# Bucket-masked attention and two MoE blocks on one core: the second block's inner layer in two parts, the first part woven into the second batch's MoE

## The chip, the cores and the metric

One core of a Trainium2 chip runs the whole program. The metric is the device time of one execution in microseconds. Engines: TensorE (PE), VectorE (DVE), ScalarE (ACT), GpSimd (POOL), SyncE (SP, which only issues DMAs here).

## The reference

Three stages, in float32:

```python
# 1. attention; q, k, v: (2, 8, 768, 64); proj: (64, 6)
bucket(t) = sum(2**i * (t @ proj > 0)[i])               # 6 sign bits of q and k
mask   = bucket(q)[:, :, :, None] == bucket(k)[:, :, None, :]
scores = where(mask, q @ k.T / 8, -1e9)
attn   = softmax(scores) @ v                            # -> x: (2, 768, 512)
# 2. first MoE; w_in (512, 1024), w_spatial (768, 768), w_out (512, 512)
u, v   = split(relu(x @ w_in))
v_s    = w_spatial @ layernorm(v) + b_spatial           # over the sequence
x      = (u * v_s) @ w_out
# 3. second MoE; w_ch1 (512, 2048), w_ch2 (2048, 512)
out    = x + relu(layernorm(x) * g_ln @ w_ch1) @ w_ch2
```

The weights w_in, w_out, w_ch1 and w_ch2 arrive as float64.

## The kernel before

Every product that must be exact to float32 is made of three matmuls: an operand is split into a high and a low part in the format fp32r, and high x high, high x low and low x high are summed in PSUM (`mm3`, `PASSES`). The high part is a copy (ScalarE or GpSimd), the low part a subtraction (VectorE or GpSimd).

**Attention.** 96 tiles of 128 queries: two batches, eight heads, six tiles (three groups of two). `attn_step(i)` is a software pipeline: transposes of tile i, scores of tile i+2, masked maximum (VectorE) and exponential (ScalarE) of tile i+1, low parts of tile i (`e_lo`), weighted sum of the group before. The transposed exponentials come in two halves of three blocks: ScalarE copies the high part and VectorE subtracts, or, where `ES` says so for the second half, ScalarE copies to `es` and GpSimd makes both parts. Score tiles lie in two buffers of two PSUM banks, 384 columns in each; four more banks (`ps_b`) serve all else. Heads come in pairs; a pair's q and k are loaded, split, masked and copied nine to zero steps ahead (`pair_stages`, `AT`). SP issues all DMAs, in order.

**Conversions.** A float64 weight piece of 512 KB is loaded into a staging buffer (`stage_f64`, tag f64), and turned into fp32r halves: one ScalarE operation (line 103), five VectorE operations (104 to 108), GpSimd's join (112), ScalarE's high half (81) and GpSimd's low half (87). There is one staging buffer in the attention and two after it. The twelve pieces of w_in and w_out are made at the steps in `CONV_AT`, stored and reloaded for the second batch; the 32 pieces of w_ch1 and w_ch2 (`w1_piece`, `w2_piece`) later.

**First MoE** (`moe1`), a generator with 24 yields: six token tiles, 12 projections of 12 matmuls, then for each of six row tiles 18 spatial matmuls (pg), the gate (gt, VectorE), four transposes (ptr_g), and 12 output matmuls (py); each y is stored to DRAM. The first batch's runs inside the attention from step `M0` on; the second batch's follows the attention, with eight PSUM banks, and between its yields the first 11 conversions and the first LayerNorm chunk are put in as `SEQ` and `LNX` say.

**Second MoE.** Three chunks of 512 tokens (chunk 0, 1, 2). In step (c, f), f of 16, `up` makes 12 matmuls into pc, ScalarE the relu and VectorE the low part of ch; `down`, one step behind, makes 12 matmuls into four sums that stay open for a chunk. The remaining 21 conversions are put in two a step. At a chunk's end VectorE adds the residual and SP stores.

The framework that builds the program orders each engine's instructions by priority (the order in which they are written) and by its own estimate of when each is ready; every engine then runs its list in order. `issue_after` puts instructions behind a given one on its engine.

Of the kernel before, what the change touches and what calls it, by code (L numbers as in the profile page):

```python
# [17 lines left out]
P = 128  # L18
# [11 lines left out]
def attn_moe_kernel(ctx: ExitStack, tc: tile.TileContext, qT, kT, v, proj, w_in, w_spT, b_sp, w_out, g_ln, w1, w2, out):  # L30
# [13 lines left out]
    TB = 5  # L44
# [3 lines left out]
    CONV_AT = (4, 9, 14, 19, 24, 30, 34, 39, 55, 60, 66, 71)  # L48
# [4 lines left out]
    M0 = 50  # L53
    SPP = [(0, t) for t in range(6)]
    VNP = [(0, t) for t in range(6)]
    LNF = 7
# [4 lines left out]
    WARM = 28  # L61
    WARM2 = 16
    XB = 3
    AT = (-9, -8, -7, -4, 0)
    ES = (1, 0)
    SEQ = (2, 2, 4, 0, 2, 0, 0, 2, 0, 2, 0, 0, 0, 0, 1, 1, 0, 2, 3, 1, 0, 0, 1, 0)
    LNX = (14, 15, 19, 22)
# [6 lines left out]
    TCH = 512  # L74
    SCALE = 1.0 / float(D) ** 0.5
# [110 lines left out]
    def w_piece(src, nk, n, nm, lo, hl=None):  # L186

        st = mp.tile([P, nk, n], F32, tag="wst", name=f"wst_{nm}", bufs=1)
        nc.sync.dma_start(out=st, in_=src)
# [14 lines left out]
    def pair_load(b, r, which=(("k", kT), ("q", qT))):  # L204

        pr = pairs.setdefault((b, r), {})
        for nm, src in which:
            pr[nm] = ap.tile([P, 2, S], F32R, tag=nm + "2", name=f"{nm}2_{b}_{r}", bufs=1 if nm == "k" else 2)
            nc.sync.dma_start(
                out=pr[nm][:, LOW[nm]].bitcast(F32), in_=src[b, 2 * r : 2 * r + 2].rearrange("h d s -> (h d) s")  # L210
            )

    def pair_split(b, r, first=False):

        for nm in "kq":
            t = pairs[b, r][nm]
            hi, lo = t[:, 1 - LOW[nm]], t[:, LOW[nm]]
            raw = lo.bitcast(F32)
# [5 lines left out]
            if nm == "k" and not first:  # L224
                split_lo(lo, raw, hi)
# [3 lines left out]
    def mismatch(b, r):  # L229
# [3 lines left out]
        for c in range(2):  # L233
            csl = slice(c * KC, (c + 1) * KC)
            pm = ps_b.tile([P, 512], F32, tag="b", name=f"pm_{b}_{r}_{c}")
            for i, nm in enumerate("kq"):
                raw = pairs[b, r][nm][:, LOW[nm]].bitcast(F32)
# [48 lines left out]
    def scores(b, h, g, j):  # L286
# [3 lines left out]
        sc = ps_s.tile([P, 2, 512], F32, tag="sc", name=f"sc_{jm}")  # L290
        for c in range(2):
            for i, rows in enumerate((P, MR)):
                nc.tensor.matmul(  # L293
                    sc[:, c, :KC],
                    qs[:rows, i, qsl],
                    ks[:rows, i, c * KC : (c + 1) * KC],
                    start=(i == 0),
                    stop=(i == 1),
# [3 lines left out]
    def masked_max(b, h, g, j):  # L302
# [6 lines left out]
            x.rearrange("p (c k) -> p c k", c=2),  # L309
            t["sc"][:, :, :KC],  # L310
# [14 lines left out]
    def transposes(b, h, g, j):  # L325
# [7 lines left out]
        for c in range(2):  # L333
# [5 lines left out]
            if c == 1 and ES[(h * NTH + g * GRP + j) % len(ES)]:  # L339
                es = ap.tile([P, 3, P], F32, tag="es", name=f"es_{jm}", bufs=1)  # L340
# [136 lines left out]
    def conversions(pieces):  # L477

        res = []
        for key, nk, n, parts in pieces:  # L480
            for i, (src, ksl, fsl) in enumerate(parts):
# [11 lines left out]
                def finish(d=d, key=key, nk=nk, n=n, ksl=ksl, fsl=fsl, done=i == len(parts) - 1):  # L493
# [4 lines left out]
                    if done:  # L498
                        w_split[key] = dram.tile([P, 2, nk, n], F32, tag=f"ws_{key}", name=f"ws_{key}")
                        nc.sync.dma_start(out=w_split[key], in_=hl.bitcast(F32))  # L500
# [9 lines left out]
    def moe1(b, ps_m, tag):  # L510
# [84 lines left out]
        for t in range(NQT + 1):  # L595
# [15 lines left out]
            if t > 0:  # L611
# [7 lines left out]
                y = mp.tile([P, DM], F32, tag="tmp", name=f"y_{b}_{t - 1}", bufs=TB)  # L619
# [9 lines left out]
    ps_s = att.enter_context(tc.tile_pool(name="ps_s", bufs=2, space=PSUM))  # L629
    ps_b = att.enter_context(tc.tile_pool(name="ps_b", bufs=4, space=PSUM))  # L630
# [4 lines left out]
    pair_load(0, 0)  # L635
# [14 lines left out]
    for i in range(-1 - QA, NT + 3):  # L650
        attn_step(i)
        for e in pair_steps.get(i, ()):
            e()
# [8 lines left out]
        if i == M0:  # L662
            m0 = moe1(0, ps_b, "b")
        if m0 is not None:
            while n0 < (i - M0 + 1) * 24 / (NT - M0):
                next(m0, None)
                n0 += 1
    for _ in m0:
        pass
    att.close()  # L670
    N1A, N2A = 8, 3
    TPC = TCH // P
    NCH = B * S // TCH
    outv = out.rearrange("b (t p) d -> (b t) p d", p=P)
    w1t, w2t, xhs, accs, chs, xcs, mvs, rs = {}, {}, {}, {}, {}, {}, {}, {}

    def w1_piece(pool, f):
        w1t[f] = pool.tile([P, 2, KFT, P], F32R, name=f"w1t_{f}", bufs=1)
        load_f64(w1t[f][:, 0], w1t[f][:, 1], w1[:, :, f * P : (f + 1) * P], f"w1_{f}")

    def w2_piece(pool, f):
        w2t[f] = pool.tile([P, 2, 1, DM], F32R, name=f"w2t_{f}", bufs=1)
        load_f64(w2t[f][:, 0], w2t[f][:, 1], w2[:, f : f + 1, :], f"w2_{f}")

    def ln_stats(c, t):
        if t == 0:
            xcs[c] = [m2a.tile([P, DM], F32, tag="xc", name=f"xc_{c}_{i}", bufs=TPC) for i in range(TPC)]
            mvs[c] = m2a.tile([P, TPC, 2], F32, tag="mv", name=f"mv_{c}", bufs=2)
        xc = xcs[c][t]
        nc.sync.dma_start(out=xc, in_=y_dram[c * TPC + t])  # L690
# [9 lines left out]
    def ln_x(c, t, pool, ps, tag):  # L700
# [144 lines left out]
```

## Time and profile before

| | |
|---|---|
| median of 3 runs | 766.64 us (763.05 to 768.99) |
| profiled execution | 762.6 us |
| its span | 760.8 us |
| mean granted TensorE clock | 0.975 |
| TensorE, VectorE, ScalarE, GpSimd busy | 91%, 63%, 45%, 38% |
| instructions | 10493 |

The span is from the first to the last event that the profiler records; the execution's own time has 1.8 us more around it. Busy shares are means over stages with different limits. Rows of matmuls overlap, since they are pipelined, so their busy times exceed what they cost; the distance from start to start is what one costs.

### The profile page before, as it was taken

How to read it: one execution, taken by the hardware profiler on the slowest of the kernel's cores; microseconds unless marked ns; L12 is line 12 of the kernel's file. 1: busy time of each engine (PE TensorE's matmuls, PEld its weight loads, DVE VectorE, ACT ScalarE, POOL GpSimd, SP SyncE). 2: the span in 40 equal slices, each digit the busy share in tenths (PEclk: the TensorE clock that was granted, in tenths of full speed). 3: DMA queues.
4: the chain of work that ended last, by engine and by line, in shares of the span. 5: the costliest groups of instructions: out<-in, count | busy, mean ns of one | idle time of the engine just before them, and what ended most of it. 6: DMA issues, size and time to landing. Idle time of an engine off the chain costs nothing.

```text
span 760.8 us, 10493 instructions
## 1 busy us (share of the span) xinstructions
PE 692.0 (91%) x3588; PEld 578.2 (76%) x3588; DVE 482.1 (63%) x889; ACT 340.1 (45%) x679; POOL 291.8 (38%) x303
## 2 busy tenths in 40 slices
PE   5989888889989999999988887997899999999997
PEld 4877767778878978897766665865678888888885
DVE  2799989884978785564499895699974114221112
ACT  1777868584665865555345432333241112110110
POOL 3367665746565784232034453555542000000000
PEclk9999999999999999999999998998899999999999
DMA  7556755462434454332713543233343000130001
GB/s 204 136 136 197 197 139 171 123 191 74 121 90 123 115 178 112 81 131 98 265 63 132 193 138 112 86 102 92 109 134 115 1 0 6 51 112 0 1 0 56
DMA packets 53095, 83.36 MB, mean 110 GB/s; under 512 B 7114, under 2 KB 36350, under 8 KB 51506
## 3 DMA queue, kind: packets, MB, share of 16 engines
q1 hardware_dynamic: 53042, 82.69, 36.6%
q8 instruction: 29, 0.48, 0.3%
q14 instruction: 24, 0.20, 0.1%
HBM read 50.08 MB, written 12.58 MB: 82 GB/s over the span
## 4 chain that ended last, share of the span: by engine, by line
PE 35%; DVE 13%; DMA 6%; issue 3%; POOL 3%; ACT 2%; DVEq 0%; ACTq 0%; POOLq 0%
PE acc L763 14%; PE pc L447 13%; DMA f_w<-in_w 4%; DVE f_w L106 2%; POOL f64c_w L112 2%; PE py L447 2%; PE pg L447 2%; DVE f64c_w L105 1%; DVE f64c_w L104 1%; DVE f64c_w L108 1%; PE po L366 1%; PE pv L447 1%; DVE f64c_w L107 1%; PE pt L337 1%; PE sc L293 1%
## 5 line engine op out<-in xcount | busy, mean ns | idle before, releaser
L447 PE MATMUL pc<-xh,w1t 128*128 128x512 f32 x576 | 146.2, 404 | 10.0 <-DVE ch L754 9.3
L763 PE MATMUL acc<-w2t,ch 128*128 128x512 f32 x576 | 141.9, 394 | 0.3 <-POOL w2t L87 0.2
L447 PEld LDWEIGHTS pc<-xh,w1t 128*128 128x128 f32 x576 | 110.8, 194 | 37.8 <-DVE ch L754 11.5
L763 PEld LDWEIGHTS acc<-w2t,ch 128*128 128x128 f32 x576 | 108.5, 189 | 25.4 <-POOL w2t L87 1.1
L754 DVE SCALAR_TENSOR_TENSOR ch<-pc,ch 128x512 fp32r<-128x512 f32 x48 | 33.0, 688 | 138.9 <-ACT ch L753 138.9
L293 PE MATMUL sc<-ks,qs 128*128 128x384 f32 (+1 forms) x384 | 93.9, 367 | 19.9 <-DVE x L308 11.5
L308 DVE TENSOR_SCALAR_CACHE_REDUCE x<-sc 128x768 f32<-128x768 f32 x96 | 90.9, 947 | 28.2 <-PE pt L337 18.7
L321 ACT ACTIVATE x<-x,nb 128x768 f32<-128x768 f32 x96 | 90.0, 937 | 37.2 <-DVE x L308 36.6
L753 ACT ACTIVATE ch<-pc 128x512 fp32r<-128x512 f32 x48 | 28.6, 596 | 157.7 <-PE pc L447 139.0
L337 PE MATMUL pt<-ident,x 128*128 128x128 f32 x576 | 85.3, 276 | 5.0 <-DVE m L239 4.0
L293 PEld LDWEIGHTS sc<-ks,qs 128*128 128x128 f32 (+1 forms) x384 | 65.2, 194 | 28.5 <-DVE x L308 18.8
L337 PEld LDWEIGHTS pt<-ident,x 128*128 128x128 f32 x576 | 69.2, 142 | 13.7 <-DVE m L239 4.7
L354 DVE TENSOR_TENSOR el<-pt,eh 128x384 fp32r<-128x384 f32 x144 | 76.2, 548 | 4.9 <-ACT eh L346 3.9
L346 ACT ACTIVATE eh<-pt 128x384 fp32r<-128x384 f32 x144 | 65.0, 488 | 29.4 <-PE pt L337 28.4
L447 PE MATMUL pv<-w_in,act_x 128*128 128x512 f32 x288 | 72.0, 401 | 3.8 <-DVE act_x L84 2.7
L112 POOL TENSOR_TENSOR f64c_w<-f_w,f64c_w 128x512 f32<-128x512 f32 x32 | 45.0, 1407 | 73.9 <-DVE f64c_w L108 54.2
L447 PEld LDWEIGHTS pv<-w_in,act_x 128*128 128x128 f32 x288 | 54.2, 192 | 15.7 <-DVE act_x L84 3.1
L87 POOL TENSOR_TENSOR el<-es,eh 128x384 fp32r<-128x384 f32 x48 | 50.1, 1043 | 3.1
L78 POOL TENSOR_SCALAR eh<-es 128x384 fp32r<-128x384 f32 x48 | 26.7, 555 | 63.7 <-ACT es L341 63.4
L366 PE MATMUL po<-eh,vs 128*128 128x256 f32 x288 | 46.4, 297 | 4.7 <-ACT eh L346 2.0
L366 PE MATMUL po<-el,vs 128*128 128x256 f32 x288 | 47.1, 290 | 0.0
L103 ACT ACTIVATE f64c_w<-f_w 128x512 f32<-128x512 f32 x32 | 21.5, 674 | 53.6 <-DMA f_w<-in_w 52.3
(121 smaller groups left out, 996.4 us busy)
## 6 DMA issues: line engine op xcount, KB each, us to landing
f_w<-in_w SPq DMA_DIRECT2D x32, 512.0 KB
ks<-k SPq DMA_DIRECT2D x48, 192.0 KB
qs<-q SPq DMA_DIRECT2D x144, 64.0 KB
wst_sp<-in_w_spT SPq DMA_DIRECT2D x12, 384.0 KB
f_in<-in_w_in SPq DMA_DIRECT2D x8, 512.0 KB
ws_in<-w_in SPq DMA_DIRECT2D x4, 1024.0 KB
w_in<-ws_in SPq DMA_DIRECT2D x4, 1024.0 KB
k<-in_kT SPq DMA_DIRECT2D x8, 384.0 KB
```

Source lines behind the costliest of these rows:

```text
L87: nc.gpsimd.tensor_tensor(dst, src, hi.bitcast(F32), op=ALU.subtract)
L112: nc.gpsimd.tensor_tensor(cf, tf, cf, op=ALU.add)
L293: nc.tensor.matmul(sc[:, c, :KC], qs[:rows, i, qsl], ks[:rows, i, c * KC : (c + 1) * KC], start=(i == 0), stop=(i == 1),)
L308: last["max"] = nc.vector.tensor_scalar(x.rearrange("p (c k) -> p c k", c=2), t["sc"][:, :, :KC], MASKED, FMAX, op0=ALU.min, op1=ALU.min, ...
L321: last["exp"] = nc.scalar.activation(t["x"], t["x"], AF.Exp, bias=t["nb"], scale=-1.0, accum_out=z_sum[b][:, n, h : h + 1]).ins
L337: nc.tensor.transpose(pt[:, i, :], t["x"][:, kt * P : (kt + 1) * P], ident)
L346: nc.scalar.activation(eh, pt, AF.Copy)
L354: nc.vector.tensor_tensor(gr["el"][:, sl, qsl], t["pt"][c], gr["eh"][:, sl, qsl].bitcast(F32), op=ALU.subtract)
L366: nc.tensor.matmul(po[:, :GW], w, gr[e][:, kt, :], start=(n == 0), stop=(n == len(parts) - 1))
L447: mm = nc.tensor.matmul(ps, lh(i), rh(j), start=(n == 0), stop=(n == tot - 1)).ins
L754: last["lo"] = nc.vector.scalar_tensor_tensor(ch[:, 1], pc, 0.0, ch[:, 0].bitcast(F32), op0=ALU.max, op1=ALU.subtract).ins
L763: last["mm"] = nc.tensor.matmul(accs[c][t], ch[:, i, t * P : (t + 1) * P], w2t[f][:, j, 0, :], start=(f == 0 and n == 0), stop=(f == NF2 - ...
```

## The change

- **Scores**: one tile of three PSUM banks for a group of two; a query tile's 768 columns are 512 + 256 (first) or 256 + 512 (second), and the middle bank is shared. `ps_b` has five banks.
- **Attention's second halves**: in the first batch all of them go through `es` and GpSimd (`ES` is now by batch), in the second one of two as before; two `es` buffers.
- **First pair**: raw q and k in tiles of their own. Later pairs: the low part of k in two halves. Fewer warm-up transposes.
- **Conversions and M0 later**: `CONV_AT` and `M0` below.
- **DMAs from ScalarE**: staging loads, spatial weight loads and the stores of converted weights.
- **Second MoE in two parts**: chunk 0 with f from 0 to 4 is put between the yields of the second batch's MoE (with ten conversions and the LayerNorm statistics of chunks 0 and 1); then chunk 1 with the same five, chunk 2 with all 16, and chunks 1 and 0 with the other eleven, their partial sums added to the residual tile on the way. The other 22 conversions follow two a step from the sixth step on. The second batch's MoE has two PSUM banks, up two, the sums four. The last chunk's y stay in SBUF.

```diff
-    TB = 5
+    TB = 4
-    CONV_AT = (4, 9, 14, 19, 24, 30, 34, 39, 55, 60, 66, 71)
+    CONV_AT = (20, 26, 32, 38, 43, 48, 52, 56, 62, 67, 72, 77)
-    M0 = 50
+    M0 = 60
-    WARM = 28
-    WARM2 = 16
+    WARM = 24
+    WARM2 = 12
-    ES = (1, 0)
+    ES = ((1,), (1, 0))
...
     def stage_f64(src, nm):
-        nc.sync.dma_start(out=st, in_=src)
+        nc.scalar.dma_start(out=st, in_=src)
...
     def pair_split(b, r, first=False):
             if nm == "k" and not first:
-                split_lo(lo, raw, hi)
+                for c in range(2):
+                    csl = slice(c * KC, (c + 1) * KC)
+                    split_lo(lo[:, csl], raw[:, csl], hi[:, csl])
...
     def scores(b, h, g, j):
-        sc = ps_s.tile([P, 2, 512], F32, tag="sc", name=f"sc_{jm}")
-        for c in range(2):
+        if j == 0:
+            groups[b, h, g]["sc"] = ps_s.tile([P, GRP, S], F32, tag="sc", name=f"sc_{jm}")
+        sc = groups[b, h, g]["sc"][:, j]
+
+        for csl in (slice(0, 512), slice(512, S)) if j == 0 else (slice(0, S - 512), slice(S - 512, S)):
...
-    ps_s = att.enter_context(tc.tile_pool(name="ps_s", bufs=2, space=PSUM))
-    ps_b = att.enter_context(tc.tile_pool(name="ps_b", bufs=4, space=PSUM))
+    ps_s = att.enter_context(tc.tile_pool(name="ps_s", bufs=1, space=PSUM))
+    ps_b = att.enter_context(tc.tile_pool(name="ps_b", bufs=5, space=PSUM))
...
-    ps_n = moe_psum.enter_context(tc.tile_pool(name="ps_n", bufs=8, space=PSUM, reuse_waits="tile"))
+    ps_n = ctx.enter_context(tc.tile_pool(name="ps_n", bufs=2, space=PSUM, reuse_waits="tile"))
+    ps_c = ctx.enter_context(tc.tile_pool(name="ps_c", bufs=2, space=PSUM, reuse_waits="tile"))
+    ps_y = ctx.enter_context(tc.tile_pool(name="ps_y", bufs=TPC, space=PSUM, reuse_waits="tile"))
+    runs = [(0, 0, NA), (1, 0, NA), (2, 0, NF2), (1, NA, NF2), (0, NA, NF2)]
+    cf = [(c, f, f == at, f == to - 1) for c, at, to in runs for f in range(at, to)]
...
+    def second(n):
+        if n < len(cf):
+            up(*cf[n][:2])
+        if 1 <= n <= len(cf):
             down(*cf[n - 1])
+
+    fill = {}
+    for n, e in (
+        *((t // 2, lambda t=t: ln_stats(0, t)) for t in range(TPC)),
+        (2, lambda: w1_piece(0)),
+        *((3, lambda t=t: ln_x(0, t)) for t in range(TPC)),
+        (4, lambda: w2_piece(0)),
+        (5, lambda: w1_piece(1)),
+        (7, lambda: second(0)),
+        (8, lambda: w2_piece(1)),
+        (10, lambda: w1_piece(2)),
+        (12, lambda: second(1)),
+        (13, lambda: w2_piece(2)),
+        (14, lambda: w1_piece(3)),
+        (15, lambda: second(2)),
+        (16, lambda: w2_piece(3)),
+        (17, lambda: w1_piece(4)),
+        (18, lambda: w2_piece(4)),
+        *((19, lambda t=t: ln_stats(1, t)) for t in range(TPC)),
+        (20, lambda: second(3)),
+        (22, lambda: second(4)),
+    ):
+        fill.setdefault(n, []).append(e)
...
+    for t in range(TPC):
+        ln_x(1, t)
+    for c in range(NCH):
+        residual(c)
+    for t in range(TPC):
+        ln_stats(2, t)
+    for t in range(TPC):
+        ln_x(2, t)
+    for f in range(NA, NF2):
+        todo.append(lambda f=f: w1_piece(f))
+        todo.append(lambda f=f: w2_piece(f))
+    for n in range(NA, len(cf) + 1):
+        second(n)
         for _ in range(2):
             if todo:
                 todo.pop(0)()
```

## Rows read from the trace of the kernel before

**Rows 1.** The page, busy tenths of TensorE in 40 slices of the span.

```profile
PE   5989888889989999999988887997899999999997
```

**Rows 2.** Stages: length; PE, PEld, DVE, ACT, POOL busy (count); clock, DMA share, GB/s.

```profile
0.00:20.40 20.40, 11.13 (x57) 9.77 (x58) 3.86 (x6) 2.97 (x3) 6.62 (x29) 0.89 0.76 196
20.40:158.90 138.50, 120.47 (x787) 105.75 (x786) 125.75 (x250) 101.95 (x225) 86.59 (x94) 0.98 0.58 163
158.90:367.50 208.60, 198.04 (x1200) 173.63 (x1199) 144.12 (x292) 131.06 (x278) 103.99 (x111) 0.99 0.41 115
367.50:469.70 102.20, 85.99 (x368) 66.07 (x366) 84.41 (x147) 41.80 (x72) 37.99 (x28) 0.95 0.47 158
469.70:577.00 107.30, 97.75 (x400) 77.33 (x401) 85.66 (x132) 37.92 (x63) 53.20 (x40) 0.94 0.30 96
577.00:755.60 178.60, 178.60 (x786) 145.63 (x784) 36.42 (x63) 24.41 (x41) 3.40 (x3) 1.00 0.09 30
```

**Rows 3.** Timeline of TensorE, 307 to 309 us (start, length, operation).

```profile
307.18 0.49 PE L337 MATMUL pt<-ident,x 128*128 128x128 f32 x3
307.53 0.97 PE L293 MATMUL sc<-ks,qs 128*128 128x384 f32 x4
308.35 0.87 PE L366 MATMUL po<-eh,vs 128*128 128x256 f32 x6
309.06 0.87 PE L366 MATMUL po<-el,vs 128*128 128x256 f32 x6
```

**Rows 4.** Timeline of the start, VectorE, SP and TensorE.

```profile
8.15 0.98 DVE L227 SCALAR_TENSOR_TENSOR k<-k 128x768 fp32r<-128x768 f32 x1 [8.15 <-PE warm L641]
...
14.06 1.10 SPq L262 DMA_DIRECT2D ks<-k  x2
...
18.80 4.93 PE L293 MATMUL sc<-ks,qs 128*128 128x384 f32 x16 [7.72 <-DMA qs<-q]
```

**Rows 5.** Groups by form: low parts, maximum (count, busy us, mean ns, idle before).

```profile
L308 DVE TENSOR_SCALAR_CACHE_REDUCE x<-sc 128x768 f32<-128x768 f32 x96 | 90.9, 947 | 28.2 <-PE pt L337 18.7 <-PE sc L293 9.0
...
L354 DVE TENSOR_TENSOR el<-pt,eh 128x384 fp32r<-128x384 f32 x144 | 76.2, 548 | 4.9 <-ACT eh L346 3.9
...
L87 POOL TENSOR_TENSOR el<-es,eh 128x384 fp32r<-128x384 f32 x48 | 50.1, 1043 | 3.1
...
L78 POOL TENSOR_SCALAR eh<-es 128x384 fp32r<-128x384 f32 x48 | 26.7, 555 | 63.7 <-ACT es L341 63.4
```

**Rows 6.** Groups of VectorE, 469.7 to 577 us.

```profile
L106 DVE SCALAR_TENSOR_TENSOR f_w<-f_w,f64c_w 128x512 uint32<-128x512 uint32 x19 | 21.7, 1144 | 0.4
L108 DVE SCALAR_TENSOR_TENSOR f64c_w<-f_w,f64c_w 128x512 f32<-128x512 uint32 x19 | 13.1, 687 | 0.4
L107 DVE TENSOR_SCALAR f64c_w<-f_w 128x512 uint32<-128x512 uint32 x19 | 11.5, 604 | 0.4
L104 DVE TENSOR_SCALAR f64c_w<-f64c_w 128x512 f32<-128x512 f32 x19 | 11.3, 597 | 11.6 <-ACT f64c_w L103 11.6
L105 DVE TENSOR_SCALAR f64c_w<-f64c_w 128x512 uint32<-128x512 uint32 x19 | 11.1, 587 | 0.4
L754 DVE SCALAR_TENSOR_TENSOR ch<-pc,ch 128x512 fp32r<-128x512 f32 x16 | 10.9, 683 | 10.1 <-ACT ch L753 10.0
```

**Rows 7.** Timeline of GpSimd and VectorE around 146 us.

```profile
146.17 1.99 POOL L87 TENSOR_TENSOR k<-k 128x768 fp32r<-128x768 f32 x1
...
146.53 2.18 DVE L108 SCALAR_TENSOR_TENSOR f64c_in<-f_in,f64c_in 128x512 f32<-128x512 uint32 x1
```

**Rows 8.** Waits of TensorE, 20.4 to 158.9 us (total, times, longest).

```profile
PE sc L293 <- DVE x L308: 7.7, 13, 1.3
```

**Rows 9.** Timeline of TensorE, 514 us.

```profile
514.75 5.49 PE L447 MATMUL pc<-xh,w1t 128*128 128x512 f32 x12 [2.55 <-DVE ch L754]
```

**Rows 10.** Busy time, 514 to 521 us, columns as in rows 2.

```profile
514.00:521.00 7.00, 6.25 (x15) 4.95 (x16) 6.31 (x11) 2.34 (x4) 3.89 (x3) 0.51 0.26 76
```

**Rows 11.** Waits of SP's DMA queue, 469.7 to 577 us.

```profile
SPq L94 <- POOL f64c_w L112: 82.0, 17, 9.8
```

More of the change, by code (lines that the diff above doesn't have):

```diff
@@ L188, in w_piece @@
         st = mp.tile([P, nk, n], F32, tag="wst", name=f"wst_{nm}", bufs=1)
-        nc.sync.dma_start(out=st, in_=src)
+        with ExitStack() as pins:
+            if "late" in last:
+                pins.enter_context(tc.issue_after(last["late"]))
+            nc.scalar.dma_start(out=st, in_=src)
         if hl is None:
@@ L217, in pair_split @@
             hi, lo = t[:, 1 - LOW[nm]], t[:, LOW[nm]]
-            raw = lo.bitcast(F32)
+            raw = pairs[b, r][nm, "raw"]
             scale = -SCALE if nm == "q" else 1.0
@@ L634, in attn_moe_kernel @@
             nc.tensor.transpose(warm, ident, ident)
-    pair_load(0, 0)
+    pair_load(0, 0, first=True)
     mismatch(0, 0)
@@ L652, in attn_moe_kernel @@
         for e in pair_steps.get(i, ()):
-            e()
+            with tc.issue_after(last["exp"]):
+                e()
         if i == 2:
@@ L663, in attn_moe_kernel @@
             m0 = moe1(0, ps_b, "b")
+            last["late"] = last["exp"]
         if m0 is not None:
+            last["late"] = last["exp"]
             while n0 < (i - M0 + 1) * 24 / (NT - M0):
@@ L755, in up, with down @@
         chs[c, f] = ch
-    def down(c, f):
+    def down(c, f, start, stop):
         ch = chs.pop((c, f))
-        if f == 0:
-            accs[c] = [ps_y.tile([P, 512], F32, tag="py", name=f"acc_{c}_{t}") for t in range(TPC)]
+        if start:
+            accs[c] = [ps_y.tile([P, 512], F32, tag="py", name=f"acc_{c}_{f}_{t}") for t in range(TPC)]
         for t in range(TPC):
@@ L773, in down @@
                 nc.vector.tensor_tensor(ot, accs[c][t], ot, op=ALU.add)
-                nc.sync.dma_start(out=outv[c * TPC + t], in_=ot)
-    ots = {}
+                if f == NF2 - 1:
+                    nc.sync.dma_start(out=outv[c * TPC + t], in_=ot)
     def residual(c):
-        ots[c] = [m2a.tile([P, DM], F32, tag="xc", name=f"ot_{c}_{t}", bufs=TPC) for t in range(TPC)]
+        ots[c] = [m2.tile([P, DM], F32, name=f"ot_{c}_{t}", bufs=1) for t in range(TPC)]
         for t in range(TPC):
@@ new lines, in attn_moe_kernel @@
+    m1 = moe1(1, ps_n, "m")
+    for n in range(24):
+        with tc.high_priority(offset=HP):
+            next(m1, None)
+        for e in fill.get(n, ()):
+            with tc.issue_after(last["moe"]):
+                e()
+    for _ in m1:
+        pass
+    moe.close()
+    m2 = ctx.enter_context(tc.tile_pool(name="m2", bufs=1, side="right", reuse_waits="tile"))
+    for t in range(TPC):
[4 more added lines that the diff above has]
+        ln_stats(2, t)
```

142 lines of the change are left out of this document (54 added, 88 removed).

## The prediction

> **What bounds the kernel now.** I read the slices of the page first [rows 1]: TensorE is near full from slice 9 to the end of the attention and from slice 29 on, and has holes in the first nine slices and in slices 18 to 28. The table by stage [rows 2] says how large they are. In the stage from 577 us on, 786 matmuls took 178.6 us: 0.227 us each with nothing lost, which is the floor for a 512-column matmul. By that floor the second batch's MoE (its 324 matmuls of 512 columns and 44 transposes at some 0.11 us: 78 us) lost 24 of its 102.2 us, and the stage behind it (384 and 16: 89 us) lost 18 of 107.3. In both VectorE is busy for 80% or more. For the attention the floor comes from a dense piece [rows 3]: start to start, three transposes in 0.35, four score matmuls in 0.82, six weighted ones in 0.71, so a tile of six, four and six costs 2.23 us, about 2.3 with its share of mask and normalising matmuls. The first batch ran 48 tiles in 138.5 us, 2.89 each: 28 us above the floor, with VectorE at 91% (125.75/48 = 2.62 us a tile), ScalarE at 2.12 and GpSimd at 1.80. The stage of the second batch is near its floor already: 48 x 2.3 + 79 (the first MoE) = 189 of 208.6. The start costs 20.4 us. So some 100 us of this span are holes in TensorE, and no matmul of weight is added or taken away: the change is worth what it does to the holes.
>
> **The change, part by part.**
>
> *Start.* The first score began at 18.80, held by DMA: the low half of k left at 14.06 although its subtraction ended at 9.1, and that subtraction, at 8.15, had itself waited for TensorE, since it overwrites the raw k that the mask matmuls read [rows 4]. With the raw tile apart, it can follow ScalarE's high half; eight warm-up transposes fewer and the w_in and spatial loads out of the first microseconds add to it. What is late next is the q copies and the mask. I take 4 us off; the bounds are 0 and 8 (the 8.15 us for which VectorE stood).
>
> *First batch.* All 48 tiles now send half of the low part over GpSimd, where 24 did: VectorE loses 24 x 0.548 = 13.2 us and GpSimd gains 24 x (0.555 + 1.043) = 38.4 us [rows 5]. ScalarE's copy only changes its target: nothing. Conversions begin at step 20 and not 4, so of the eight pieces that lay in this stage some 5.5 remain; a piece costs VectorE 1.144 + 0.687 + 0.604 + 0.597 + 0.587 = 3.62 us [rows 6]: 9 us less. VectorE then has 125.75 - 13.2 - 9 = 103.6 us, 2.16 a tile. GpSimd has 86.6 + 38.4 = 125 less a few for the moved pieces, about 2.5 a tile: it becomes the fullest engine, above TensorE's 2.3. Now 2.62 a tile on the fullest engine ran at 2.89; GpSimd is less tightly in the loop (maximum, exponential and transposes don't pass through it), so I take 2.5 + 5% = 2.62 a tile: 126 us, 12 us less. Bounds: 2.4 a tile (-23) and the rival below (+32). The split of k's low part into halves lies in that: the whole one took 1.99 us, and VectorE's operation beside it 2.18, where its like takes 0.687 [rows 6, 7], so a half frees VectorE about a microsecond earlier, in seven pairs.
>
> *Scores in three banks.* A pair of tiles shares the middle bank, so the first scores of a pair wait for both maxima of the last pair, not for one; in return there is a fifth bank for transposes and sums. In the first batch TensorE already waits 7.7 us for maxima, in 13 places [rows 8]. Behind such a wait stand transposes and weighted sums in TensorE's order. One full maximum is 0.947 us [rows 5], but a pair has 5.2 us of other TensorE work and the loop from maximum to maximum (scores of both 1.64, maxima 2 x 0.95, some 0.3 of handing over) is 3.9: it should fit. I charge 3 us for 48 pairs, between -4 (the fifth bank) and the rival below.
>
> *Second batch.* M0 at 60 packs the same MoE into 36 tiles and not 46; 12 tiles go without filler but with three conversions: VectorE there some 2.9 us a tile by the rows above: 35 us, 7 over the floor. The other 36 tiles and the MoE (83 + 79 = 162) I take at 8% over their floor, 175 (the stage now is 10% over, and part of that is its first tiles without the MoE). Sum 210 against 208.6: +1, from -10 to +12.
>
> *MoE of the second batch with five parts of chunk 0 inside.* TensorE's floor is 78 + 5 x 24 x 0.227 = 105 us. VectorE's load is about that of now (84.4): one piece fewer (-3.6), the second LayerNorm's statistics more (+8), five ch rows (+3.4 [rows 6]): 92 us. TensorE is now the longer one and has other matmuls while it waits for gate or act_g: 116 us. A new wait stands against it: this MoE had eight PSUM banks and now has two, so TensorE's third block waits until ScalarE or VectorE has read the first, and all matmuls queue behind that. Its 30 blocks (12 projections, six each of pg, ptr, py) cost between nothing and one reading row each (0.683, as ch [rows 6]), 0 to 20 us; most of these reads are needed by the next block anyway, so I take 4. That makes 120; now the same work takes 102.2 + 27.3 = 129.5: 9 less, from -22 (107, near the floor) to +7 (136).
>
> *Conversions behind it.* 22 pieces remain, and the longest run, chunk 2, stands where they are needed, so the last is due 109 us after the MoE and not 87 us. That helps only if need was the limit. The rows say otherwise: TensorE waited 2.55 us for ch, whose VectorE row stands in order behind conversion rows, and the next 12 matmuls took 5.49 us where the floor is 2.73, at a granted clock of 0.51, the lower of the two levels (1.2 GHz) [rows 9, 10]. The chain through two staging buffers gave 19 pieces in 107.3 us [rows 2, 6], 5.6 us each, while TensorE did 16 steps; two pieces are queued a step, as before. Scaled to 22 pieces the hole is 21 us; for the later due times and a freer SP I take 5 off. 16 against now 18: -2, from -12 to +12.
>
> *DMAs from ScalarE.* SP stood 82 us in 17 waits for the staging buffer, released by GpSimd's join [rows 11]; ScalarE would now stand there. But ScalarE's own next row, the high half of the same piece, waits for the same join, so the wait costs it nothing new, and SP's stores and loads no longer stand behind it; the issue itself, 0.55 us a DMA in SP's row [rows 4], falls on an engine at 35 to 41% [rows 2]. Zero; if ScalarE came there early, relu, ch and the next down stand behind it, which is part of the rival on conversions. The Trainium skill ("DMA: Bandwidth & Descriptors", section "Issuing engines are not separate DMA queues") says that another issuing engine saves only issue time, since all use the same 16 DMA engines. By it this part gives nothing at all; the row agrees, as the wait was for a buffer.
>
> *Seams.* The two further run changes each drain four sums (0.68 us each, eight adds more) before the next run's first down: +1 each. At the MoE's end the new pool waits for the old one's last readers and eight blocks of transposes stand before the first up: +3. Together +5, from 2 to 10. The tail is unchanged.
>
> **Sum.** -4 -12 +3 +1 -9 -2 +5 = -18: a span of 743 us. The profiled execution took 762.6 us, 1.8 above its span, and lies 0.5% under the median of 766.64; so 744.8 for such an execution and 749 for a median. Since the parts have more room below than above (100 us of holes, 18 of them taken), I say 745.
>
> **Rivals.**
> 1. *GpSimd becomes the bound of the first batch* (slower). Today it stands idle 52 of 138.5 us there. If its idle time remains, because it waits for ScalarE's copies in order, the stage takes 118 + 52 = 170 us: +44 on the forecast, 789. It decides (slower than before) once more than 30 of these 52 us stay (a stage of 148). For it: it is the fullest engine by the sum. Against it: its results are needed only at the weighted sum, a tile later, from double buffers.
> 2. *The order of the conversions behind the MoE costs more*. If half of the 22 pieces go two to a step, 5.5 steps (30 us) last 11 x 5.6 = 62 us, and the hole is some 36 us and not 16: 765. For it: the step in rows 9 looks like that. Against: over the whole stretch 19 pieces now cost 18 us only.
> 3. *The shared bank holds the scores*: a whole maximum (1.03 us with its read-out) in each of the 24 pairs of the first batch: 745 + 25 = 770. The rows of the waits now, 0.6 us each in 13 places, speak against that size.
> 4. *The holes nearly fill*: the woven MoE near its floor (107), the first batch at 2.4 a tile, conversions at their floor less a few: 745 - 13 - 11 - 6 = 715.
> 5. *VectorE loses to GpSimd what it was relieved of*. Some 28 conversion operations of the first batch, each held back by at most one low part of 1.043 us, are 29 us on VectorE: 133 us, 2.77 a tile, and at 5% above it the stage takes 139: 745 + 13 = 758. Rows 7 show one such delay, of 1.5 us; of the conversion operations' means only that of line 106 is far above its neighbours [rows 6], so I give it little. The Trainium skill ("SBUF — State Buffer", section "Who interferes with whom") states the mechanism and so speaks against this part: a VectorE instruction with two SBUF inputs and a GpSimd one that reads SBUF share a port, and the second is blocked whole. Rows 7 agree.
>
> **How the numbers follow.** About 1% (7.7 us) is what runs of this kernel can tell from no change. Forecast 0.57 (own range 727 to 762), rivals 1 to 5: 0.09, 0.12, 0.06, 0.11, 0.05. The range 716 to 770 leaves out rival 1, half of rival 4 and the edges. Faster (under 759): most of the forecast (0.51), rival 4 (0.11), and parts of rivals 2 and 5 (0.05): 0.67; same 0.20; slower 0.13.
>
> **What would show it.** First score near 15. Maxima of the first batch 2.6 us apart, GpSimd above 85% and VectorE under 85% there. Few TensorE waits for a maximum over 0.5 us. Between the last projections and the last output of the second MoE, up and down in the places where gate and act_g are awaited, granted clock at 1.0. In the 110 us behind it still waits for ch with a clock under 0.95; no wait for w1t or w2t. The prediction is wrong if GpSimd paces the first batch, if the last stretch is smooth, or if ScalarE shows long waits ahead of relu.

## The result and the profile after

The changed kernel takes 746.62 us (median of 4 runs, 745.25 to 748.01) where the kernel before, run beside it, took 766.21: a ratio of 0.9746, 95% interval 0.9703 to 0.9788. The prediction was 745 with a range of 716 to 770. The profiled execution took 745.25 us, its span 743.5; the forecast was a span of 743. The total is right, but several of its terms are not.

The page of the kernel after, the engines' busy time and the slices of TensorE and GpSimd, beside [rows 1]:

```profile
PE 688.4 (93%) x3580; PEld 567.5 (76%) x3580; DVE 468.0 (63%) x873; ACT 339.1 (46%) x679; POOL 333.9 (45%) x358
...
PE   7899988899899998999889999799988999999996
...
POOL 2788898998586672421035233235444400000000
```

The holes of the first nine slices are a little smaller, GpSimd is busy for 70% or more from the second of them on, and behind the attention TensorE's slices under 90% are now 20, 21, 26, 30 and 31.

The table by stage of the kernel after, columns as in [rows 2]. Its cuts: first maximum, end of the first batch, of the attention, first `up` of chunk 1, last conversion, last matmul:

```profile
0.00:13.40 13.40, 11.34 (x52) 9.16 (x52) 4.22 (x7) 2.97 (x3) 4.86 (x26) 1.00 0.62 152
13.40:145.70 132.30, 116.99 (x792) 100.24 (x793) 106.80 (x213) 99.31 (x220) 113.38 (x136) 1.00 0.59 156
145.70:356.80 211.10, 199.10 (x1192) 169.63 (x1190) 150.42 (x304) 133.07 (x283) 122.41 (x127) 0.98 0.46 132
356.80:484.20 127.40, 114.42 (x502) 91.59 (x501) 89.95 (x183) 50.66 (x86) 40.71 (x30) 0.95 0.41 138
484.20:595.60 111.40, 104.47 (x433) 81.55 (x434) 92.07 (x133) 38.18 (x64) 52.58 (x41) 0.97 0.31 98
595.60:738.30 142.70, 142.10 (x617) 115.29 (x615) 23.29 (x36) 14.93 (x25) 0.00 (x0) 1.00 0.04 15
```

Against before, in us. The MoE's row holds the same work in both kernels. The changed kernel has five ups, five downs and the 16 transposes of chunk 1 there, which before came later; in the column of before they are moved from the last row to this one, at 24 matmuls of 0.227 us a step (27.3) and some 0.11 us a transpose (1.8).

| stage | before | after | difference | forecast |
|---|---|---|---|---|
| to the first maximum | 20.4 | 13.4 | -7.0 | -4 |
| both batches of the attention | 347.1 | 343.4 | -3.7 | -8 |
| second batch's MoE, five steps and 16 transposes, with its seam | 131.3 | 127.4 | -3.9 | -6 |
| the rest, to the last matmul | 256.8 | 254.1 | -2.7 | 0 |
| sum (the tail is 5.2 in both) | | | -17.3 | -18 |

The profiled execution of before was at the low end of its runs, so these differences add up to a little less than the medians' 19.6.

What TensorE waited for in the first batch of the kernel after (total, times, longest), against 7.7 us in 13 places for the maximum in [rows 8]:

```profile
PE po L372 <- POOL eh L77: 4.9, 6, 1.1
...
PE sc L303 <- DVE x L314: 1.5, 2, 0.9
```

The waits of the scores (sc) for the maximum are nearly gone, in spite of the shared bank; in their place the weighted sums (po) wait 4.9 us for GpSimd's halves. In the woven MoE (first fence) and behind it (second) TensorE's waits are these (px_c are the LayerNorm's transposes, ptr_g those of the gate):

```profile
PE pv L453 <- DMA w_in<-ws_in: 3.5, 1, 3.5
PE px_c L732 <- ACT xc L722: 2.2, 1, 2.2
PE px_c L732 <- DVE mv L167: 2.2, 1, 2.2
PE ptr_g L440 <- DVE gt L613: 1.2, 1, 1.2
```

```profile
PE acc L751 <- DVE ch L742: 6.1, 6, 2.5
PE pc L453 <- DVE xh L735: 3.0, 1, 3.0
```

Inside the MoE, waits for the gate are down to 1.2 us. Before they were:

```profile
PE ptr_g L434 <- DVE gt L607: 8.0, 5, 2.1
```

The largest that are left stand at its edges: the reload of w_in at its start, and the LayerNorm and transposes (px_c, xh) of the next chunk at its end. The changed kernel's MoE in two stretches, columns as in [rows 2], shows the same. The first holds most of the projections, and no up or down is woven into it:

```profile
356.80:398.00 41.20, 34.87 (x138) 27.57 (x137) 27.86 (x73) 16.30 (x29) 9.91 (x8) 0.88 0.41 140
398.00:478.00 80.00, 78.33 (x358) 63.17 (x356) 56.43 (x102) 29.41 (x49) 27.01 (x19) 1.00 0.37 124
```

Where something is woven in, TensorE is busy for 78.3 of 80 us at full clock. The losses lie in the 41 us ahead and in the 6 us behind. Behind the MoE TensorE still waits for `ch`, as [rows 9] showed.

### The profile page after: what moved, and what is told of

The parts are those of the page before. It is cut to its first block, busy times and chain, and to the rows that moved or that the text cites. A ratio compares the mean times of both kernels' runs of the same rounds, so it can differ in the third digit from the quotient of the medians.

```text
span 743.5 us, 10402 instructions
## 1 busy us (share of the span) xinstructions
PE 688.4 (93%) x3580; PEld 567.5 (76%) x3580; DVE 468.0 (63%) x873; ACT 339.1 (46%) x679; POOL 333.9 (45%) x358
## 4 chain that ended last, share of the span: by engine, by line
PE 49%; DVE 16%; DMA 11%; POOL 11%; issue 6%; ACT 5%; SPq 1%; ACTq 0%; DVEq 0%; POOLq 0%
PE acc L751 12%; PE pc L453 11%; PE pv L453 6%; DMA f_w<-in_w 5%; PE sc L303 4%; PE pg L453 4%; PE po L372 4%; PE pt L343 3%; POOL el L86 3%; PE py L453 2%; DMA wst_sp<-in_w_spT 2%; DVE f_w L105 2%; POOL f64c_w L111 2%; DVE f64c_w L107 2%; POOL eh L77 1%
## 5 line engine op out<-in xcount | busy, mean ns | idle before, releaser
L751 PE MATMUL acc<-w2t,ch 128*128 128x512 f32 x576 | 145.3, 397 | 6.9 <-DVE ch L742 6.1
L303 PE MATMUL sc<-ks,qs 128*128 128x512 f32 (+3 forms) x384 | 83.8, 353 | 8.0 <-issue 4.5
L86 POOL TENSOR_TENSOR el<-es,eh 128x384 fp32r<-128x384 f32 x72 | 78.3, 1089 | 3.0
L453 PE MATMUL pv<-w_in,act_x 128*128 128x512 f32 x288 | 75.6, 418 | 4.1 <-DMA w_in<-ws_in 3.5
L360 DVE TENSOR_TENSOR el<-pt,eh 128x384 fp32r<-128x384 f32 x120 | 64.0, 548 | 22.6 <-ACT eh L352 18.1
L453 PEld LDWEIGHTS pv<-w_in,act_x 128*128 128x128 f32 x288 | 56.6, 201 | 17.3 <-DMA w_in<-ws_in 4.0
L303 PEld LDWEIGHTS sc<-ks,qs 128*128 128x128 f32 (+1 forms) x384 | 57.3, 192 | 15.3 <-issue 5.6
L352 ACT ACTIVATE eh<-pt 128x384 fp32r<-128x384 f32 x120 | 56.1, 487 | 27.7 <-PE pt L343 26.3
L372 PE MATMUL po<-eh,vs 128*128 128x256 f32 x288 | 52.0, 304 | 7.1 <-POOL eh L77 4.9
L77 POOL TENSOR_SCALAR eh<-es 128x384 fp32r<-128x384 f32 x72 | 41.5, 579 | 36.9 <-ACT es L347 36.9
L372 PEld LDWEIGHTS po<-eh,vs 128*128 128x128 f32 x288 | 39.7, 190 | 13.2 <-POOL eh L77 7.3
```

Of the source, the lines that this page charges most:

```text
L77: nc.gpsimd.tensor_scalar(dst, src, 1.0, 0.0, op0=ALU.mult, op1=ALU.add)
L86: nc.gpsimd.tensor_tensor(dst, src, hi.bitcast(F32), op=ALU.subtract)
L303: nc.tensor.matmul(sc[:, csl], qs[:rows, i, qsl], ks[:rows, i, csl], start=(i == 0), stop=(i == 1))
L352: nc.scalar.activation(eh, pt, AF.Copy)
L360: nc.vector.tensor_tensor(gr["el"][:, sl, qsl], t["pt"][c], gr["eh"][:, sl, qsl].bitcast(F32), op=ALU.subtract)
L372: nc.tensor.matmul(po[:, :GW], w, gr[e][:, kt, :], start=(n == 0), stop=(n == len(parts) - 1))
```

## The experiments

Ratios are to the kernel before, run on the same chip in the same rounds. Each edit is made in the kernel after, or in the kernel before where the section says so. The change itself was not run in those rounds. An edit in the kernel after is compared with a kernel of the same rounds that came out within 1 us of the change: es_half (746.54), conv_old (747.26) or todo15 (746.1).

Four kernels, the change, no_weave, todo15 and no_weave_pin, write the attention alike. Their first batches took 132.3, 133.0, 135.3 and 135.8 us, their second ones 211.1, 209.8, 211.7 and 210.6. So a first batch can differ by 3.5 us between two profiles without an edit in it.

### GpSimd's share of the first batch: es_half

```diff
-    ES = ((1,), (1, 0))
+    ES = ((1, 0), (1, 0))
```

> The changed kernel with every second low part of the first batch back on VectorE (as before the change); all else changed. The stage of the first batch takes 132.3 us in the changed kernel, with GpSimd busy 113.4 and VectorE 106.8. If relieving VectorE is what gained there, the stage goes back towards 138 us and the time up by about 6, to some 752. If GpSimd has become the bound of that stage, as rival 1 had it in a mild form, the stage gets shorter, to about 126, and the time falls to about 740. Equal (within 3 us) if the two limits lie level.

746.54 us, ratio 0.9711 (0.9661 to 0.976): the same as the change. The first batch in its table by stage:

```profile
13.50:142.20 128.70, 114.85 (x789) 99.67 (x790) 111.95 (x235) 98.90 (x220) 78.26 (x93) 1.00 0.60 159
```

GpSimd has 35 us less, VectorE 5 more, and the stage is 3.6 us shorter, not longer; the second batch is 2.1 longer (213.2). Moving 24 more halves to GpSimd therefore bought nothing; whether it cost something in its own stage, 3.6 us can't show.

### Conversions and MoE where they were: conv_old

```diff
-    CONV_AT = (20, 26, 32, 38, 43, 48, 52, 56, 62, 67, 72, 77)
+    CONV_AT = (4, 9, 14, 19, 24, 30, 34, 39, 55, 60, 66, 71)
-    M0 = 60
+    M0 = 50
```

> The changed kernel with the old places of the first twelve conversions and M0 at 50. My steps: the first batch gets 2.5 pieces more on VectorE (9 us) but has some room there, +2 to +6; the second batch gets the MoE spread over ten more tiles, 0 to -8. Sum within 4 us of the changed kernel. If the later places are what relieved the first batch, +8 or more; if they are what costs the second batch (211 us, more than the 208.6 before the change, though banks and start gained), the time falls below 740.

747.26 us, 0.9735 (0.9697 to 0.9773): the same. The two batches:

```profile
12.40:156.90 144.50, 123.85 (x793) 105.85 (x793) 118.56 (x230) 103.82 (x227) 128.18 (x146) 0.95 0.58 166
156.90:359.90 203.00, 194.65 (x1190) 170.12 (x1189) 140.75 (x288) 129.60 (x275) 105.31 (x117) 0.98 0.44 121
```

Against the change the first batch is 12.2 us longer, where I expected 2 to 6, and the second 8.1 shorter. Later conversions relieve the first batch by more than I expected, and the second pays most of it back. The 12 us are probably not the conversions' alone: b_sc3, below, has them at the early places too, with GpSimd's half share, and ran this stage in 133.3 us. Here GpSimd is busy for 128.18 of 144.5.

### The banks: b_sc3, sc4, psb4

b_sc3 is the kernel before with the three score banks and the fifth bank of `ps_b` alone. sc4 is the kernel after with scores in two buffers of two banks and four for the rest. psb4 keeps the three score banks and leaves one bank idle:

```diff
-    ps_b = att.enter_context(tc.tile_pool(name="ps_b", bufs=5, space=PSUM))
+    ps_b = att.enter_context(tc.tile_pool(name="ps_b", bufs=4, space=PSUM))
```

> The kernel before the change with scores in three banks and five banks for the rest, and nothing else changed. Putting four banks back into the changed kernel cost about 9 us, 14 of them in the attention. If that is the layout's own worth, this kernel is 8 to 14 us faster than the one before, all in the attention (347 us from the first maximum to the end). My step had it 3 us slower. If it only helps together with the later conversions or GpSimd's larger part, within 3 us.

> The changed kernel with scores in two buffers of two banks and four banks for the rest, as before the change. If the shared middle bank costs TensorE waits (my charge was 3 us), the attention gets shorter by 2 to 4 us and the wait of scores for a maximum, 1.5 us in the first batch of the changed kernel, stays near that. If the fifth bank for transposes and sums is what helps, the scores' wait for maxima goes back towards 7.7 us in the first batch and the time up by 4 to 8 us.

> The changed kernel with scores in three banks but only four banks for the rest (one bank of eight lies idle). If the fifth bank is what the new layout gives, the time goes to that of four and four banks: 5 to 9 us up. If it is the scores' layout itself (512 and 256 columns, one row of 768 to read), the time stays within 3 us of the changed kernel.

- b_sc3: 757.57 us, 0.9878 (0.9855 to 0.99), so 9 us faster than before by this alone. Its first batch takes 133.3 us where before took 138.5 and the whole change 132.3.
- sc4: 755.92, 0.9814 (0.9766 to 0.9861), 9.4 us above es_half. I had expected the scores' waits for maxima to go back towards 7.7 us in the first batch if it is the fifth bank that helps; they are 1.5 us, as in the change.
- psb4: 756.81, 0.9873 (0.9826 to 0.992), 10.7 us above todo15.

The batches of b_sc3:

```profile
22.50:155.80 133.30, 121.11 (x794) 101.94 (x795) 122.15 (x248) 100.48 (x224) 83.02 (x92) 0.98 0.58 160
155.80:362.70 206.90, 196.35 (x1190) 169.38 (x1188) 148.04 (x294) 130.39 (x279) 106.35 (x112) 0.98 0.43 120
```

Those of psb4, and of todo15 from the same rounds:

```profile
13.10:152.20 139.10, 121.23 (x789) 103.09 (x789) 105.22 (x215) 99.59 (x221) 113.40 (x138) 0.96 0.55 148
152.20:370.80 218.60, 200.17 (x1193) 170.76 (x1193) 149.77 (x302) 134.23 (x283) 117.43 (x125) 0.98 0.44 127
```

```profile
12.80:148.10 135.30, 120.48 (x792) 103.94 (x793) 107.81 (x214) 99.02 (x220) 113.28 (x136) 0.96 0.58 153
148.10:359.80 211.70, 198.99 (x1191) 169.53 (x1190) 150.25 (x304) 133.04 (x283) 122.52 (x127) 0.98 0.46 132
```

psb4 is sc4's picture (140.0 and 217.5) with the other layout of the scores. So what the kernel loses in sc4 isn't the layout but the fifth bank. Against todo15 psb4 has 3.8 us more in the first batch and 6.9 in the second; the first of these is hardly more than equal attentions differ by. Of the total the bank is worth 8 to 11 us in the three kernels, by ratios and medians. In sc4, on the banks of before, the attention takes 357.5 us where before took 347.1: there the other edits of the attention cost some 10 us. With the new banks they cost 3 (340.2 in b_sc3, 343.4 in the change).

Where the bank acts is seen in part. In before's first batch TensorE has, besides [rows 8], this row of waits:

```profile
PE pt L337 <- DVE m L239: 4.0, 3, 2.1
```

The transposes (pt) don't read the mask m; VectorE reads its matmuls' bank for it, one of the four of `ps_b`. With five banks this row is gone; b_sc3 has 1.0 us of the kind left, ahead of weighted sums. In psb4's second batch (total, times, longest):

```profile
PE pt L343 <- DVE el L360: 3.6, 2, 2.7
...
PE pg L453 <- DVE xT L378: 1.6, 2, 0.9
```

Here too neither operation reads what VectorE wrote; both wait for a bank to be read out, and the change has neither row in this stage. These rows are 5.2 us, where the stage has 6.9 to 7.5 more than todo15 and the change. In psb4's first batch there is little of the kind, and before has 1.6 us beyond the 4.0 in its first batch and 0.2 in its second. So that one bank more is worth this much is shown by three kernels that agree; how it acts is shown for half of it or less. One run speaks for caution: mid55, below, has five banks and nearly psb4's stages.

### The weave: no_weave, no_weave_pin, b_ps2

no_weave wrote the five steps behind the MoE; no_weave_pin also holds them there, behind the MoE's last matmuls:

```diff
-        (7, lambda: second(0)),
...
-        (22, lambda: second(4)),
...
+    for n in range(NA):
+        with tc.issue_after(last["py"]):
+            second(n)
```

> The changed kernel with the five up and down steps of chunk 0 behind the second batch's MoE and not between its yields; conversions, LayerNorm places and PSUM banks as in the changed kernel. If the weave fills holes of the MoE (my step: 9 us less), the MoE ends some 15 us earlier than the 477 us of the changed kernel, but the five steps cost 27 us behind it: the time goes up by 9 to 12 us. If the weave gains nothing, since what it puts in only lengthens a stage that is set by VectorE and by the start of its weights, the time stays within 3 us.

> As no_weave, with the five steps of chunk 0 now held behind the last output matmul of the second batch's MoE on TensorE (in no_weave the builder's order had pulled them forward again, so it told nothing). If the weave fills holes, the MoE alone ends near 465 to 470 us of its span (before the change it took 102 us), and the five steps come behind it, so the stage up to the first up of chunk 1 is 10 us or more longer than the 127 us of the changed kernel and the time some 757. If the holes are elsewhere (in the projections, which wait for weights and have nothing woven in), within 4 us.

no_weave: 747.29, 0.9718 (0.9667 to 0.977). It tells nothing: the framework drew the steps forward into the MoE again (first `up` at 404 us, in the change at 406). no_weave_pin: 755.68, 0.9857 (0.9831 to 0.9884), 8.4 us above conv_old. Its MoE and the five steps behind it:

```profile
359.10:464.00 104.90, 88.94 (x368) 69.27 (x367) 85.77 (x165) 41.55 (x71) 38.34 (x27) 0.92 0.44 145
464.00:503.80 39.80, 30.56 (x138) 24.21 (x136) 34.51 (x52) 15.80 (x27) 18.73 (x14) 0.92 0.51 176
```

Together 144.7 us, 17.3 more than the woven 127.4. The second row holds five ups, five downs and the 16 transposes of chunk 1: 120 x 0.227 + 16 x 0.11 = 29, so 11 us are lost at the seam, of which the waits for `xh` ahead of the transposes are the plainest. These transposes don't read `xh`; VectorE reads one of their two PSUM banks for it:

```profile
496.69 0.77 PE L732 MATMUL px_c<-ident,xc 128*128 128x128 f32 x4 [3.64 <-DVE xh L735]
...
501.04 1.09 PE L732 MATMUL px_c<-ident,xc 128*128 128x128 f32 x4 [3.57 <-DVE xh L735]
```

Of the 17 us some 10 come back, because the conversions go on meanwhile. The joins of GpSimd (length of the stretch, busy time, count) in no_weave_pin, ahead of chunk 1 and behind its first `up`:

```profile
359.10:503.80 144.70, 26.44 (x18) 0.92 0.46 153
503.80:610.00 106.20, 19.17 (x14) 0.97 0.19 60
```

and in the change:

```profile
356.80:484.20 127.40, 17.85 (x12) 0.95 0.41 138
484.20:595.60 111.40, 26.86 (x20) 0.97 0.31 98
```

Unwoven, 18 pieces are done by then, woven 12. Behind the seam no_weave_pin waits for no `ch` at all and needs 244.2 us to its last matmul, the change 254.1. The weave's profit is what is left of the two, 8.4.

b_ps2 is the kernel before with two PSUM banks for the second batch's MoE (and two for the LayerNorm transposes) where it had eight:

> The kernel before the change with two PSUM banks for the second batch's MoE (and two for the transposes of the LayerNorm chunk that lie in it) and not eight. My step charged 4 us for the two banks, from 0 to 20. If the readers are mostly needed by the next block anyway, the MoE's 102 us grow by less than 4 and the time stays within 4 us; if TensorE lived from running ahead, the MoE gets 10 us or more longer.

769.8 us, 1.0043 (1.0016 to 1.007): 3.3 us slower, where I had charged 4. Its MoE shows a wait that before lacks, the spatial matmuls for the reading of a bank:

```profile
PE pg L447 <- ACT y L620: 6.0, 4, 2.8
```

### The issuing engine: dma_sp, b_act

dma_sp puts the staging, spatial and conversion DMAs of the kernel after back on SP; b_act puts those of the kernel before on ScalarE.

```diff
-        nc.scalar.dma_start(out=st, in_=src)
+        nc.sync.dma_start(out=st, in_=src)
```

> The changed kernel with staging loads, spatial weight loads and the stores of converted weights issued by SP again. My step said zero, since the wait is for a staging buffer: the time stays within 3 us and the pieces behind the MoE keep their 5 us spacing. The rival: SP's queue held them up behind its other waits, then the pieces come later and the stretch behind the MoE is 5 us or more longer.

> The kernel before the change with its staging loads, spatial weight loads and stores of converted weights issued by ScalarE and nothing else changed. The run of the changed kernel with SP issuing them began its first maximum 5.5 us later, with two bulk loads at 3.4 and 4.0 us ahead of the copies of q and k. If that is what holds the start, the first maximum comes near 15 us here and not at 20.5, and the time falls by 4 to 7 us. If the start is held by the raw tile that k's low part overwrites, it stays near 20 us and the time within 3 us.

b_act: 768.76 us, 1.0013 (0.999 to 1.0037), nothing, though its first score comes at 16.21 and not at 18.80 as in [rows 4], and its first maximum at 17.9, between the two places that I had expected. dma_sp: 753.63, 0.9795 (0.9752 to 0.9839), 7.1 us above es_half. Most of that is the start: its first maximum comes at 18.9 us, the change's at 13.4. The timeline of SP and TensorE there:

```profile
3.40 0.54 SPq L93 DMA_DIRECT2D f_in<-in_w_in  x1
3.98 0.43 SPq L191 DMA_DIRECT2D wst_sp<-in_w_spT  x1
...
16.00 2.90 PE L303 MATMUL sc<-ks,qs 128*128 128x512 f32 x8 [5.23 <-DMA qs<-q]
```

On SP the two large loads are issued ahead of the copies of k and q, which land late. In the change neither is issued in the first 20 us: the first load of w_in comes at 68.0, the first spatial one at 259.9. Both are held behind an exponential by `issue_after`, and the exponential is ScalarE's, so this holds them only where ScalarE issues them. For the spatial loads that is an edit of the change too, though its description doesn't name it. b_act lacks it, and there ScalarE issues the spatial load ahead of all copies:

```profile
0.73 0.43 ACTq L189 DMA_DIRECT2D wst_sp<-in_w_spT  x1
```

So b_act takes only the load of w_in out of the start. The change's start:

```profile
5.65 0.96 DVE L234 SCALAR_TENSOR_TENSOR k<-k_raw,k 128x768 fp32r<-128x768 f32 x1 [5.65 <-ACT k L226]
...
10.98 0.47 PE L303 MATMUL sc<-ks,qs 128*128 128x512 f32 x1
```

k's low part begins 2.5 us earlier than in [rows 4] and waits for ScalarE, no longer for TensorE.

### The order behind the MoE, and a version between: todo15, mid55

todo15 lets conversions in at three per two steps, not four. mid55 takes every other tile's second half from GpSimd in the first batch, M0 = 55 and conversions between the old and the new places:

```diff
-        for _ in range(2):
+        for _ in range(1 + n % 2):
```

```diff
+    CONV_AT = (12, 18, 24, 29, 35, 40, 46, 51, 58, 64, 69, 74)
+    M0 = 55
+    ES = ((1, 0), (1, 0))
```

> The changed kernel with the last 22 conversions put in three to two steps and not four to two. If the order in VectorE's list (two pieces a step ahead of ch) makes the hole behind the MoE, it shrinks by some 5 us of about 15, and the time falls by 3 to 6 us. If the chain through the two staging buffers sets the pace whatever the order (5.3 us a piece), nothing moves, or the last pieces come late and the time rises.

> The changed kernel with every second low part of the first batch on VectorE and M0 and the first conversions half way between the old and the new places (M0 at 55). The late places made the first batch 12 us shorter and the second 8 us longer than the old ones in the profiles; if part of the first gain can be had without the second loss, 740 to 744. If the two move together, as one TensorE floor would have it, 746 again.

todo15: 746.1 us, 0.9753 (0.9698 to 0.9808), no change. GpSimd's joins in 102 us of the stretch, todo15 and then the change:

```profile
491.00:593.00 102.00, 26.77 (x20) 0.98 0.29 93
```

```profile
490.00:592.00 102.00, 26.84 (x20) 0.98 0.30 93
```

20 pieces in 102 us in either order. mid55: 752.42, 0.9809 (0.975 to 0.9868), 6.3 above todo15, neither of the two times that I expected. Its first batch (138.1) lies between es_half's and conv_old's, its second (219.3) above both; its profiled execution took 756.33, the longest of its four. No version beats the change; es_half and todo15 equal it.

## Why the prediction was right

The total came out because errors of both signs cancelled: the start and the last stretch gave 5.7 us more than forecast, the attention and the woven MoE 6.4 less. That the sum is so near is luck. The start's error is sure, since the nine kernels with both of its edits have their first maximum at 12.4 to 13.5 us; the other errors are of the size by which two profiles differ.

**Start: mechanism right, size too small (-7.0, said -4, bounds 0 and 8).** The step named two holders, the raw tile of k and the large loads. With the raw tile apart and the loads still in front (dma_sp) the first score comes at 16.00 and not at 18.80; with both loads gone as well (the change) it comes at 10.98, 7.8 us sooner than before. The step had them add up to 4. The loads alone weren't tried: in b_act (16.21) one of the two goes first, and k's low part still waits for TensorE.

**First batch: the size is half, and the reason is another (-6.2; said -12, and +3 for the banks in both batches).** The step "VectorE then has 125.75 - 13.2 - 9 = 103.6 us ... I take 2.62 a tile" got the engines right (VectorE 106.8, GpSimd 113.4) and failed in taking the fullest engine's time for the stage's. The tiles ran at 132.3/48 = 2.76 us. The relief by GpSimd is worth nothing (es_half), and b_sc3, which has neither it nor later conversions, runs this stage in 133.3. What shortens it there is the bank. GpSimd's full share with early conversions makes it 144.5 (conv_old), so that here the later conversions may do no more than undo what the share costs.

**Three banks: wrong sign.** "I charge 3 us ... between -4 and the rival below" set the risk of the shared bank high and that of a fifth bank low. The shared bank costs next to nothing: psb4, which has it, takes as long as sc4, which hasn't, and the scores of the first batch wait 1.6 and 1.5 us for maxima in the two. So their fall from 7.7 us isn't the layout's doing either. The loop of 3.9 us did fit, though the step's "5.2 us of other TensorE work" is the whole pair at 2.6 us a tile: by [rows 3] a pair has 2.8 us besides its scores, against 2.2 for two maxima and their handing over. The fifth bank is worth 8 to 11 us by three kernels, among the largest terms of the change and outside my bounds. A row of before would have spoken for it: the 4.0 us in which transposes waited for the reading of a mask bank. I read the waits for maxima and passed over that row, and its 4.0 us are still half or less of what the bank gives.

**Second batch: +2.5 (said +1).** Right, as the sum of two things that I did not see apart: more packed fillers and later conversions (about +8 by conv_old) and the fifth bank (-7 by psb4). In the kernel before, the bank gives less there: 206.9 in b_sc3 against 208.6.

**Woven MoE: -9 said, 8.4 measured as the worth of the weave, but the stage fell by 3.9 only.** The step priced the floor (its transposes are 40 and not 44, 0.4 us) and the two banks well (3.3 for 4), and the weave fills what it is woven into, at full clock (78.3 of 80 us). It failed at the edges. "+3" stood for a seam that costs 11 us unwoven, since the statistics of chunk 2 and the transposes of chunk 1 stand ahead of chunk 1's first `up`, with VectorE busy for 34.5 of 39.8 us. The weave covers much of it; part shows still, in the waits for `mv` and `xh` of 2.2 and 3.0 us. And the projections, for which the step has no term, took longer: 138 matmuls in 41.2 us at a granted clock of 0.88, where before this took 142 in 37.5 at 0.95:

```profile
367.50:405.00 37.50, 33.75 (x142) 27.06 (x141) 29.01 (x69) 16.23 (x28) 11.49 (x10) 0.95 0.44 153
```

The weave also takes time away from the conversions, which return it behind.

**Conversions behind: the hole was forecast at 16 us and the run changes at 2; together they are 18.1.** The matmuls from chunk 1 on are 1032 x 0.227 + 16 x 0.11 = 236.0 of 254.1 us. The same count for before, 1032 and 32, gives 258.6 - 237.8 = 20.8 lost. So the gain is 2.7, where -2 for the conversions and +2 for the run changes made nothing; two profiles can't tell that from none. From GpSimd's join of one piece to that of the next it takes 5.29 us in the 20 pieces behind the MoE, and took 5.45 in the 19 of before. What I said of the order, that the chain through two staging buffers sets the pace and not the due times, todo15 shows.

**DMAs from ScalarE: zero was right for the kernel before** (b_act, 1.0013). In the change they are worth 6 to 7 us (ratio and medians of dma_sp and es_half), 5.5 of it ahead of the first maximum, where I had counted the loads' removal under the start. It is the order and not the issue time: in the trace of dma_sp both loads go first, in the change they are held back. The Trainium skill ("DMA: Bandwidth & Descriptors", section "Issuing engines are not separate DMA queues") says that only issue time is saved; b_act as a whole agrees, and the start is where it leaves out who is issued first.

**Rivals.** 1 (GpSimd bounds the first batch) is there in traces: GpSimd is busy for 86% of it and TensorE waits 4.9 us for it; but it is nowhere near the 44 us priced. 2 (the order of the conversions) is refuted by todo15, 3 (the shared bank) by psb4 and the waits. 4 did not come true: the MoE's woven part alone is near its floor, the first batch ran at 2.76 us a tile and the hole behind is 18.1. 5 (the shared port) is small: GpSimd's two operations on a half take 1089 and 579 ns where [rows 5] had 1043 and 555, 4% more; VectorE's 106.8 us against my 103.6 leaves at most 3 us for it.

**The signs.** Most came true: maxima 2.76 us apart, GpSimd above 85% and VectorE under it in the first batch, two waits for a maximum, full clock where something is woven in, no wait for a weight tile behind it. Two missed: the first score came at 10.98 and not near 15, and the clock behind the MoE was 0.97 and not under 0.95.

**What stays open.** Why mid55 is slower than either neighbour isn't settled: its stages (138.1 and 219.3) are nearly psb4's (139.1 and 218.6), with five banks and not four. Any edit makes the framework lay out its lists anew, and single stages move by several microseconds with it, so part of what psb4 and sc4 lost may be that. Stage differences under 4 us between two profiles are therefore not evidence here. Two more edits of the change weren't tried apart: the stages of the pairs, like the spatial loads, are held behind an exponential, and `TB` is 4. That the weave is worth 8.4 us rests on one kernel, whose stages both moved.

## What to carry to other kernels

A gain on an engine's sum is not a gain on the stage: here 24 halves moved from VectorE to GpSimd, the fullest engine's load fell, and nothing came of it (es_half), while one more rotating PSUM bank gave 8 to 11 us. Before pricing a transfer between engines, look which waits are for a buffer to come free (the releaser reads a buffer that the waiting instruction is to write, and makes nothing that it reads) and price one more buffer first.

Two holders of one start have to be removed together. Work that is moved off a hole (conversions, a weave) tends to reappear as a hole where it lands: compare the two stages as one.

An experiment that only rewrites the order may not change it, when a framework schedules; look in the trace whether it did, as in no_weave, before reading its time.

## What was not expected of the hardware

The granted clock of the first batch differs between kernels that write the attention alike, at nearly the same number of matmuls (791 or 792). It was 1.00 in the change, 0.97 in no_weave and 0.96 in todo15 and no_weave_pin, with TensorE busy for 116.99, 119.76, 120.48 and 120.93 us. So psb4's 0.96 and 121.23 us there are not the bank's. These are means of a stage over the clock's two levels. What TensorE did before the clock fell in the one and not in the other wasn't looked into, and no run here settles it.
